# One TensorE piece, on alternating row halves, for the score products of both head groups of a chunk

## The chip, the cores and the metric

The kernel runs on one core of one Trainium2 chip. The metric is device time in microseconds (us) of one execution. The engines of the core work side by side and meet at semaphores: TensorE multiplies matrices (PE; its weight loads are shown apart as PEld), VectorE (DVE), ScalarE (ACT) and GpSimd (POOL) do element-wise work, and SyncE (SP) issues the transfers, which the DMA engines carry out.

## What is computed

Three layers follow one another. The first is a recurrent attention layer over 4 batches, 8 heads, 768 steps and head dimension 40. For each batch and head:

```
for t in range(S):
    m_new = maximum(f[t] + m, i[t]);  fs = exp(f[t] + m - m_new);  is_ = exp(i[t] - m_new)
    C = fs * C + is_ * outer(v[t], k[t]);   n = fs * n + is_ * k[t]
    y[t] = sigmoid(o[t]) * (C @ q[t]) / maximum(abs(n . q[t]), 1)
```

Its output, 3072 tokens by 320, goes through `((x @ w1) * (x @ w2) @ w3) @ w_out` (inner width 1024) and then through `max(x @ w1, x @ w2, x @ w3) @ w_out` (inner width 768). All is float32; the weights of the last two layers arrive as 64-bit floats and are converted on the chip.

## The kernel before

**Tiling of the first layer.** The 768 steps of a batch are cut into 9 chunks of 88 (the last has 64), and the 8 heads into 2 groups of 4. A unit `u` is one batch, one chunk and one head group: `u = 18 * b + 2 * c + g`, 72 units in all. Inside a unit the recurrence is computed in its parallel form: `s = k^T q` for every pair of steps of the chunk (`s`, 88 x 88 for each of 4 heads, in PSUM), times the decay factors `dd` (L610 writes the product into `pk`), and then `o = pk @ [v, 1, state]` (L625, in `outs`). `rest` takes the new state from `o` into `kv` of the unit two further on (L630), divides by the denominator (L643 to L646, into `y`) and multiplies by the gate (L651). When both groups of a chunk have their `y`, `x_cols` transposes it on TensorE (L666) and splits it into the high and low parts `xh` and `xl` that the second layer reads.

**Two ways of the product s.** Units below `NP = 28` use the direct way, on which the change bears: q and k of the unit arrive by one transfer as `raw`, 40 rows of data padded to 48 (L530), and four float32 matmuls with 40 rows each, one for each head, give `s` (L569); each shows as two weight loads and two matmuls in the trace. Later units split q and k into parts of lower precision and use L594; the change does not touch them.

**Buffers.** `s`, `o` (from unit 10 on) and the transposed `y` share two PSUM banks under the tag `aq`, in turn, by the order in which they are written down. `raw` has three buffers for units 0 to 9 (`raw0`) and two for the rest; those lie in a shared tile that the trace calls `misc`. A new tile waits until the old user of its buffer is done.

**The order of the work.** The program writes operations down with `P.op(engine, cost in ns, function, reads, writes)`; `Plan.run` then simulates all engines with these costs and with biases by kind of operation, and issues each engine's instructions in the order in which they start in that simulation. On the chip an engine's order is fixed: an instruction that waits holds up all behind it on its engine. That goes for SP too, which issues all transfers. The units are written down by `more()`: ten before the second layer begins (with three `fold` steps, L926, that combine two weight matrices on TensorE), then one at each of certain steps of the second and third layers (`a_step`, `b_step`, `c_step`, `d_step`, which make the long rows of L698 to L702, L765 to L769 and L784). So the units from 10 on are mixed into the matmuls of the second and third layers.

Of the kernel before, what the change touches and what calls it, by code (L numbers as in the profile page):

```python
# [8 lines left out]
F32 = mybir.dt.float32  # L9
# [7 lines left out]
B, H, S, D = 4, 8, 768, 40  # L17
L = 88
LP = 96
NCH = 9  # L20
# [8 lines left out]
NP = 28  # L29
NQ = 10  # L30
# [44 lines left out]
def act(n, psum=False):  # L75
    return (51 if psum else 93) + 0.8333 * n


def dve(n):
    return 69 + 1.0417 * n  # L80
# [200 lines left out]
def mlstm_moe_kernel(  # L281
# [21 lines left out]
    V, A, G, PE, SP = nc.vector, nc.scalar, nc.gpsimd, nc.tensor, nc.sync  # L303
    PS = bass.MemoryType.PSUM
    P = Plan()
# [41 lines left out]
    def view(t, shape, dt):  # L347
        n = 1
        for d in shape[1:]:
            n *= d  # L350
        v = t[0:shape[0], 0:n]
        if dt != F32:
            v = v.bitcast(dt)
        if len(shape) == 3:
            v = v.rearrange("p (a b) -> p a b", b=shape[2])
        elif len(shape) == 4:
            v = v.rearrange("p (a b c) -> p a b c", b=shape[2], c=shape[3])
        return v

    def new(key, shape, dt, tag):  # L360
        P.tile(key, tag, len(slots[tag]))
        made[key] = view(slots[tag][turn[tag] % len(slots[tag])], shape, dt)
        turn[tag] += 1
        if gates_done.get(tag):
            P.state[key][0][None] = gates_done[tag]
        return key

    def T(*key):
        return made[key]

    def dma(ns, fn, r=(), w=()):
        return P.op("D", ns, fn, r, w)
# [12 lines left out]
    def c3(t):  # L385
        return t.rearrange("p (c t) -> p c t", t=L)
# [21 lines left out]
    def f():  # L408
# [5 lines left out]
         r=[("g", "ff")], w=[("g", "git")])  # L414

    def f():
# [6 lines left out]
         r=[("g", "git")], w=[("g", "aug", 1)])  # L423

    def f():
# [7 lines left out]
        out=c3(T("g", "gft")), in0=c3(T("g", "gft")), in1=mp[:, 0:NCH].unsqueeze(2).to_broadcast([32, NCH, L]),  # L433
# [5 lines left out]
    for b in range(B):  # L439
        dma(141, lambda b=b: SP.dma_start(  # L440
            out=d_na[b].rearrange("c h t -> h c t"), in_=c3(T("g", "gft"))[b * 8:b * 8 + 8]
# [20 lines left out]
    for c in range(SIGN):  # L462
        dma(318, lambda c=c: SP.dma_start(out=sg0[0:LP, c], in_=og[0, c]), w=[("sg", (0, c))])
        sig.append(P.op("A", 360 + (1283 if c == 0 else 0), lambda c=c: A.activation(
            out=sg0[0:LP, c], in_=sg0[0:LP, c], func=AF.Sigmoid
# [13 lines left out]
    def ub(u):  # L479
        b, r = divmod(u, 18)  # L480
        return b, r // 2, r % 2, GL[r // 2], 128 if r > 1 else L
# [41 lines left out]
    def unit(u):  # L523
        if u < DUO:
            load(u + 2)
        b, c, g, n, r = ub(u)
        h0 = b * 8 + g * 4
        if u < NP:
            new(("raw", u), [48, 4, 2 * L], F32, "raw0" if u < NQ else "raw")
            dma(333, lambda: SP.dma_start(out=T("raw", u), in_=qk0[b, g, c]), w=[("raw", u)])  # L530
        else:
            new(("raw", u), [120, 2, 4, L], F32, "raw")
            dma(888, lambda: SP.dma_start(out=T("raw", u), in_=qk[b, g, c]), w=[("raw", u)])
        if L < r:
            new(("qq", u), [128, 4, L], F32, "qq")
            dma(174, lambda: SP.dma_start(out=T("qq", u)[80:128], in_=qk[b, g, c, 56:104, 0]),
                r=[("qqb", turn["qq"] % len(slots["qq"]))], w=[("qq", u)])
        new(("dd", u), [128, 4, n], F32, "dd")
        dma(464, lambda: SP.dma_start(
            out=T("dd", u)[:r], in_=d_na[b, c:c + 1, g * 4:g * 4 + 4, 0:n].to_broadcast([r, 4, n])  # L540
        ), r=[("dna", b)], w=[("dd", u)])
        if g == 0 and (b, c) >= (0, SIGN):
            gates(b, c)

        P.op("G", 735, lambda: G.tensor_tensor(  # L545
            out=T("dd", u)[:r], in0=am[:r, c, h0:h0 + 4].unsqueeze(2).to_broadcast([r, 4, n]), in1=T("dd", u)[:r],
            op=ALU.subtract,
        ), r=[("am", 0)], w=[("dd", u)])
        P.op("G", 460, lambda: G.affine_select(  # L549
            out=T("dd", u)[0:L], in_=T("dd", u)[0:L], pattern=[[0, 4], [1, n]], compare_op=ALU.is_ge, fill=-1e30,  # L550
            base=0, channel_multiplier=-1,
        ), w=[("dd", u)])
        P.op("A", act(4 * n) + (1283 if u == 0 else 0), lambda: A.activation(  # L553
            out=T("dd", u)[:r], in_=T("dd", u)[:r], func=AF.Exp
        ), w=[("dd", u)], after=sig)
        new(("pk", u), [128, 4, 128], F32, "pk")
        m = 128 if c < NCH - 1 else n
        if m > n:
            P.op("G", 415, lambda: G.tensor_tensor(  # L559
                out=T("pk", u)[:r, :, L:128], in0=T("kv", u)[:r, :, 0:40],  # L560
                in1=T("dd", u)[:r, :, n - 1:n].to_broadcast([r, 4, 40]), op=ALU.mult,
            ), r=[("kv", u, "k"), ("kvb", u % BUF["kv"]), ("dd", u)], w=[("pk", u, 0)])
        new(("s", u), [128, 4, n], F32, "aq")
        if u < NP:

            def f():
                raw = T("raw", u)
                for h in range(4):
                    PE.matmul(T("s", u)[:L, h], lhsT=raw[0:40, h, L:2 * L], rhs=raw[0:40, h, 0:n], start=True, stop=True)  # L569

            P.op("P", 720, f, r=[("raw", u)], w=[("s", u)])
        else:
            ks = kst[u % 2]
            new(("qs", u), [120, 4, n], F32R, "qs")
            P.op("A", act(4 * n), lambda: A.copy(out=T("qs", u), in_=T("raw", u)[:, 0, :, 0:n]),
                 r=[("raw", u)], w=[("qs", u)])
            P.op("A", act(4 * n), lambda: A.copy(out=ks, in_=T("raw", u)[:, 1]),
                 r=[("raw", u)], w=[("kst", u % 2, 1)])
            P.op("G", 889, lambda: G.tensor_tensor(
                out=T("qs", u)[0:40], in0=T("raw", u)[0:40, 0, :, 0:n], in1=T("qs", u)[0:40].bitcast(F32),  # L580
                op=ALU.subtract,
            ), r=[("raw", u)], w=[("qs", u)])
            P.op("V", dve(4 * n), lambda: V.tensor_tensor(
                out=ks[64:104], in0=T("raw", u)[64:104, 1], in1=ks[64:104].bitcast(F32),
                op=ALU.subtract,
            ), r=[("raw", u)], w=[("kst", u % 2, 1)], port=1)

            duo = u >= DUO
            if duo:
                new(("o", u - 1), [128, 4, 41], F32, "aq")  # L590

            def f():
                for h in range(4):
                    PE.matmul(T("s", u)[0:L, h], lhsT=ks[:, h], rhs=T("qs", u)[:, h], start=True, stop=True)  # L594
                if duo:
                    outs(u - 1)

            if duo:
                P.op("P", 1210, f, cols=300, r=[("qs", u), ("kst", u % 2), ("pk", u - 1), ("kv", u - 1)],
                     w=[("s", u), ("o", u - 1)])  # L600
            else:
                P.op("P", 390, f, cols=90, r=[("qs", u), ("kst", u % 2)], w=[("s", u)])
        if L < r:

            def scaled(e):
                e.tensor_tensor(out=T("pk", u)[64:128, :, 0:n], in0=T("qq", u)[64:128, :, 0:n],
                                in1=T("dd", u)[64:128], op=ALU.mult)

            P.op(("G", "V"), (889, dve(4 * n)), (lambda: scaled(G), lambda: scaled(V)), r=[("qq", u), ("dd", u)], w=[("pk", u, 1)], port=1)
        P.op("V", dve(4 * n), lambda: V.tensor_tensor(  # L610
            out=T("pk", u)[:L, :, 0:n], in0=T("s", u)[:L], in1=T("dd", u)[:L], op=ALU.mult
        ), r=[("s", u), ("dd", u)], w=[("pk", u, 1)])
        if u >= DUO:
            rest(u - 1)
            load(u + 2)
        if u + 1 < DUO or u == NU - 1:
            new(("o", u), [128, 4, 41], F32, f"ac{u % 3}" if u < 10 else "aq")
            P.op("P", 910 if m > n else 500, lambda: outs(u), cols=210, r=[("pk", u), ("kv", u)], w=[("o", u)])
            rest(u)
# [363 lines left out]
    def more():  # L983
        u = cur[0]
        if u < NU:
            unit(u)
            cur[0] = u + 1

    folds = [0]
# [75 lines left out]
def _lay(i):  # L1065
    import numpy as np

    f = np.float32
    q, k, v = i["q"], i["k"], i["v"]
    pad = lambda a: np.concatenate([a, np.zeros(a.shape[:-1] + (NCH * L - S,), f)], -1)  # L1070
    qk = np.stack([q, k], 2).reshape(B, 2, 4, 2, S, D).transpose(0, 1, 5, 3, 2, 4)
    qk = pad(qk).reshape(B, 2, D, 2, 4, NCH, L).transpose(0, 1, 5, 2, 3, 4, 6)
    eye = np.eye(D, dtype=f)
    qk0 = qk.transpose(0, 1, 2, 3, 5, 4, 6)
    qk0 = qk0.reshape(B, 2, NCH, D, 4, 2 * L)
    qk0 = np.concatenate([qk0, np.zeros((B, 2, NCH, 48 - D, 4, 2 * L), f)], 3)
    qk = np.concatenate([qk, qk[:, :, :, 0:24], qk, qk[:, :, :, 24:40]], 3)
    kvt = np.zeros((B, 2, NCH, LP, 4, 81), f)
    kvt[:, :, :, L:LP, :, 0:40] = eye[0:LP - L, None]
# [3 lines left out]
    for c in range(NCH):  # L1083
        n = GL[c]
# [58 lines left out]
```

## Time and profile before

| | |
|---|---|
| median of 3 runs | 730.17 us (728.78 to 731.63) |
| profiled execution | span 729.3 us from its first to its last instruction; its time outside the span is not in the rows |
| busy share | PE 96%, PEld 92%, DVE 60%, ACT 51%, POOL 42% |
| instructions | 12666, of them 4341 matmuls and as many weight loads |
| data moved | 78.84 MB, mean 108 GB/s |

PE busy is the time from a matmul's start to its modelled end; as they are pipelined, the pace is read from starts. Matmuls of line 569, which the change touches, start between 12.8 and 213.6 us.

### The profile page before, as it was taken

To read this page: it belongs to the slowest core of one execution; us is meant where nothing else is said; L and a number is where in the kernel's file an instruction comes from. 1 tells how busy PE (TensorE), PEld (TensorE's weight loads), DVE (VectorE), ACT (ScalarE), POOL (GpSimd) and SP (SyncE) were. 2 spreads that over 40 slices of the span, in tenths; PEclk is the share of its full clock that TensorE was granted. 3 is DMA by queue.
4 is the path that set the end of the run, shared out by engine and by line. 5 is a ranking of instruction groups with operands and counts; after the bars stand their busy time and mean duration, and the time that the engine had idled before them with its cause. 6 is when DMAs were issued, how large, how long until landed. Compare 5 with 4: busy or idle time off the path is not lost.

```text
span 729.3 us, 12666 instructions
## 1 busy us (share of the span) xinstructions
PE 699.4 (96%) x4341; PEld 674.3 (92%) x4341; DVE 437.0 (60%) x998; ACT 373.8 (51%) x697; POOL 308.3 (42%) x438
## 2 busy tenths in 40 slices
PE   1699999999999999999999999999999999999998
PEld 1677897889999999999999999999999999999998
DVE  4688876667766865866466676754747632233333
ACT  5968998689854355555343446545333222231311
POOL 1786755556646536664044456543406200000000
PEclk9978999999999999999999999999999999999999
DMA  7987887464433445543023445432305100000000
GB/s 207 251 247 226 233 230 219 146 185 157 148 88 102 117 111 148 139 124 87 12 76 85 109 121 153 113 83 69 88 1 112 49 1 27 1 1 1 1 27 28
DMA packets 50954, 78.84 MB, mean 108 GB/s; under 512 B 11882, under 2 KB 37930, under 8 KB 50890
## 3 DMA queue, kind: packets, MB, share of 16 engines
q1 hardware_dynamic: 50890, 78.04, 38.4%
q8 instruction: 34, 0.56, 0.3%
q14 instruction: 30, 0.25, 0.1%
HBM read 73.98 MB, written 4.03 MB: 107 GB/s over the span
## 4 chain that ended last, share of the span: by engine, by line
PE 84%; DMA 7%; DVE 3%; POOL 2%; issue 2%; SPq 1%; ACT 0%; POOLq 0%; DVEq 0%
PE wk L698 13%; PE wk L699 12%; PE wk L700 12%; PE ac L784 9%; PE aq L625 6%; PE wk L702 6%; PE wk L701 6%; PE ac L765 4%; PE ac L769 4%; PE wk L926 4%; PE ac L767 3%; DMA stg<-in_w3t 2%; PE aq L569 2%; PE aq L594 1%; DMA dd<-d_na 1%
## 5 line engine op out<-in xcount | busy, mean ns | idle before, releaser
L718 DVE TENSOR_TENSOR pl<-pr,ph 128x384 fp32r<-128x384 f32 (+1 forms) x91 | 60.8, 669 | 75.8 <-ACT ph L714 73.1
L714 ACT CAST ph<-pr 128x384 fp32r<-128x384 f32 (+1 forms) x114 | 57.8, 510 | 90.5 <-PE ac L784 43.9
L698 PE MATMUL wk<-xh,wch 128*128 128x384 f32 x288 | 99.5, 345 | 0.0
L700 PE MATMUL wk<-xl,wch 128*128 128x384 f32 x288 | 97.1, 337 | 0.0
L699 PE MATMUL wk<-xh,wcl 128*128 128x384 f32 x288 | 97.1, 337 | 0.0
L749 DVE TENSOR_TENSOR pr<-pr,wk 128x384 f32<-128x384 f32 (+1 forms) x98 | 52.8, 541 | 64.4 <-PE wk L702 57.8
L698 PE MATMUL wk<-xh,wah 128*128 128x384 f32 x256 | 90.9, 355 | 0.0
L718 POOL TENSOR_TENSOR pl<-pr,ph 128x384 fp32r<-128x384 f32 (+1 forms) x23 | 24.2, 1052 | 153.7 <-ACT ph L714 138.9
L699 PE MATMUL wk<-xh,wal 128*128 128x384 f32 x256 | 86.6, 338 | 0.0
L700 PE MATMUL wk<-xl,wah 128*128 128x384 f32 x256 | 86.5, 338 | 0.0
L545 POOL TENSOR_TENSOR dd<-am,dd 128x352 f32<-128x352 f32 (+2 forms) x72 | 57.5, 799 | 49.6 <-DMA dd<-d_na 48.8
L559 POOL TENSOR_TENSOR pk<-kv,dd 128x160 f32<-128x160 f32 (+1 forms) x64 | 38.7, 606 | 72.1 <-PE aq L625 64.9
L625 PE MATMUL aq<-kv,pk 128*128 128x41 f32 (+2 forms) x496 | 62.2, 275 | 2.1 <-POOL pk L559 1.4
L731 ACT COPY pr<-wk 128x384 f32<-128x384 f32 x64 | 30.5, 477 | 64.2 <-PE wk L702 64.1
L553 ACT ACTIVATE dd<-dd 128x352 f32<-128x352 f32 (+2 forms) x72 | 35.2, 492 | 52.3 <-POOL dd L549 51.7
L625 PEld LDWEIGHTS aq<-kv,pk 128*128 128x128 f32 (+2 forms) x496 | 57.4, 184 | 4.5 <-POOL pk L559 1.7
L651 POOL TENSOR_TENSOR misc<-misc 88x160 f32<-88x160 f32 (+1 forms) x62 | 41.5, 669 | 46.7 <-DVE misc L646 42.5
L746 ACT COPY pr<-wk 128x384 f32<-128x384 f32 x48 | 23.1, 482 | 70.5 <-PE wk L702 70.4
L733 DVE TENSOR_TENSOR pr<-pr,wk 128x384 f32<-128x384 f32 x64 | 35.2, 551 | 40.0 <-PE wk L702 35.7
L698 PEld LDWEIGHTS wk<-xh,wch 128*128 128x128 f32 x288 | 54.1, 188 | 0.1
L699 PEld LDWEIGHTS wk<-xh,wcl 128*128 128x128 f32 x288 | 54.2, 188 | 0.0
L700 PEld LDWEIGHTS wk<-xl,wch 128*128 128x128 f32 x288 | 54.0, 188 | 0.0
(133 smaller groups left out, 1729.5 us busy)
## 6 DMA issues: line engine op xcount, KB each, us to landing
misc<-in_qk SPq DMA_DIRECT2D x44, 330.0 KB
dd<-d_na SPq DMA_DIRECT2D x56, 176.0 KB
kv<-in_kv SPq DMA_DIRECT2D x72, 121.5 KB
stg<-in_w3t SPq DMA_DIRECT2D x13, 512.0 KB
stg<-in_wc SPq DMA_DIRECT2D x9, 512.0 KB
qq<-in_qk SPq DMA_DIRECT2D x64, 66.0 KB
misc<-in_og SPq DMA_DIRECT2D x31, 120.0 KB
out<-misc SPq DMA_DIRECT2D x23, 160.0 KB
```

The costliest lines, as they stand in the source:

```text
L545: P.op("G", 735, lambda: G.tensor_tensor(out=T("dd", u)[:r], in0=am[:r, c, h0:h0 + 4].unsqueeze(2).to_broadcast([r, 4, n]), in1=T("dd", u) ...
L625: PE.matmul(T("o", u)[:m, h], lhsT=T("pk", u)[:r, h, 0:m], rhs=T("kv", u)[:r, h, 40:81], start=True, stop=True)
L651: P.op("G", 485, lambda: G.tensor_tensor(out=yv(), in0=yv(), in1=sg(b, c).rearrange("p (h d) -> p h d", d=D)[:n, g * 4:g * 4 + 4], op=ALU.mult
L698: PE.matmul(p, lhsT=h_[:, kt], rhs=xh[:, kt], start=kt == 0, stop=False)
L699: PE.matmul(p, lhsT=l_[:, kt], rhs=xh[:, kt], start=False, stop=False)
L700: PE.matmul(p, lhsT=h_[:, kt], rhs=xl[:, kt], start=False, stop=False)
L701: PE.matmul(p, lhsT=r_, rhs=xh[:, 2], start=False, stop=False)
L702: PE.matmul(p, lhsT=r_, rhs=xl[:, 2], start=False, stop=True)
L714: P.op("A", act(n), lambda sl=sl: A.copy(out=T("ph", key)[:, sl], in_=T(*src)[:, sl]), r=[src + part], w=[("ph", key) + part])
L718: e.tensor_tensor(out=T("pl", key)[:, sl], in0=T(*src)[:, sl], in1=T("ph", key)[:, sl].bitcast(F32), op=ALU.subtract)
L749: P.op("V", dve(sl.stop - sl.start), lambda ps=ps, sl=sl: V.tensor_tensor(out=T(*sc)[:, sl], in0=T(*sc)[:, sl], in1=T(*ps)[:, sl], op=ALU. ...
L784: PE.matmul(T(f"ac{m}", (k, 1)), lhsT=src[:, m * 128:m * 128 + 128], rhs=w[:, o:o + DM], start=first_, stop=last_,)
```

## The change

One transfer now brings q and k of both head groups of a chunk: group 0 on rows 0 to 39 and group 1 on rows 64 to 103 of one tile of 104 rows, with zeros between. One TensorE piece then makes `s` of both units. It alternates between the groups: head 0 of group 0 from rows 0 to 39, head 0 of group 1 from rows 64 to 103, head 1 of group 0, and so on. Group 0 writes into one `aq` bank, group 1 into the other, and both are taken at once. The piece counts 800 in the plan, where each of the two counted 720; the transfer counts 720, where each counted 333. `more()` writes both units of a chunk down at the even call and nothing at the odd call. The number of matmuls is the same.

```diff
         if u < NP:
-            new(("raw", u), [48, 4, 2 * L], F32, "raw0" if u < NQ else "raw")
-            dma(333, lambda: SP.dma_start(out=T("raw", u), in_=qk0[b, g, c]), w=[("raw", u)])
+            if g == 0:
+                new(("raw", u), [104, 4, 2 * L], F32, "raw0" if u < NQ else "raw")
+                dma(720, lambda: SP.dma_start(out=T("raw", u), in_=qk0[b, c]), w=[("raw", u)])
...
-        new(("s", u), [128, 4, n], F32, "aq")
+        if u >= NP:
+            new(("s", u), [128, 4, n], F32, "aq")
         if u < NP:
-
-            def f():
-                raw = T("raw", u)
-                for h in range(4):
-                    PE.matmul(T("s", u)[:L, h], lhsT=raw[0:40, h, L:2 * L], rhs=raw[0:40, h, 0:n], start=True, stop=True)
-
-            P.op("P", 720, f, r=[("raw", u)], w=[("s", u)])
+            if g == 0:
+                for v in (u, u + 1):
+                    new(("s", v), [128, 4, n], F32, "aq")
+
+                def f():
+                    raw = T("raw", u)
+                    for h in range(4):
+                        for v, a in ((u, 0), (u + 1, 64)):
+                            PE.matmul(
+                                T("s", v)[:L, h], lhsT=raw[a:a + 40, h, L:2 * L], rhs=raw[a:a + 40, h, 0:n],
+                                start=True, stop=True,
+                            )
+
+                P.op("P", 800, f, r=[("raw", u)], w=[("s", u), ("s", u + 1)])
...
         if u < NU:
-            unit(u)
+            if u >= NP:
+                unit(u)
+            elif u % 2 == 0:
+                unit(u)
+                unit(u + 1)
             cur[0] = u + 1
```

The host lays q and k out to match, with 104 rows for each batch and chunk.

## Rows read from the trace of the kernel before

**Rows 1.** The page: span, and busy time by engine.

```profile
span 729.3 us, 12666 instructions
PE 699.4 (96%) x4341; PEld 674.3 (92%) x4341; DVE 437.0 (60%) x998; ACT 373.8 (51%) x697; POOL 308.3 (42%) x438
```

**Rows 2.** Windows: stretch, busy of PE, PEld, DVE, ACT, POOL, clock, DMA, GB/s.

```profile
0.00:24.00 24.00, 4.22 (x26) 3.66 (x26) 10.24 (x16) 13.50 (x19) 6.64 (x21) 1.00 0.82 221
24.00:60.00 36.00, 33.08 (x162) 28.05 (x162) 29.88 (x74) 29.15 (x43) 25.42 (x39) 0.81 0.87 246
60.00:112.00 52.00, 48.80 (x298) 43.37 (x298) 42.80 (x98) 47.44 (x76) 36.76 (x46) 0.97 0.80 227
112.00:216.00 104.00, 104.00 (x620) 93.49 (x620) 72.34 (x162) 85.68 (x145) 57.91 (x73) 1.00 0.53 158
216.00:730.00 514.00, 509.29 (x3242) 505.75 (x3241) 281.79 (x652) 198.03 (x418) 181.58 (x262) 1.00 0.26 71
```

**Rows 3.** Waits of TensorE, 60 to 112 us: us in total, times, longest.

```profile
PE aq L625 <- POOL pk L559: 1.4, 1, 1.4
PE aq L569 <- DVE kv L630: 0.8, 1, 0.8
PE aq L569 <- DMA misc<-in_qk: 0.7, 1, 0.7
PE aq L569 <- DVE pk L610: 0.3, 1, 0.3
```

**Rows 4.** Tile aq: duration ns min/median/max, first and last start.

```profile
L569 PEld LDWEIGHTS aq<-misc x144: 149/155/155, 71.0 to 213.5; 40*88 40x88 f32 x144
L569 PE MATMUL aq<-misc x144: 238/238/307, 71.0 to 213.6; 40*88 40x88 f32 x128, 40*88 40x64 f32 x16
L610 DVE TENSOR_TENSOR pk<-aq,dd x72: 412/520/524, 21.2 to 582.1; 88x352 f32<-88x352 f32 x64, 88x256 f32<-88x256 f32 x8
```

**Rows 5.** Timeline of TensorE around one unit: start, us, count at the end.

```profile
101.34 0.34 PE L702 MATMUL wk<-xl,war 128*128 128x384 f32 x1
101.61 0.85 PE L569 MATMUL aq<-misc 40*88 40x88 f32 x8
102.39 1.08 PE L625 MATMUL aq<-kv,pk 128*128 128x41 f32 x8
103.31 0.42 PE L698 MATMUL wk<-xh,wah 128*128 128x384 f32 x1
```

**Rows 6.** Timeline of the weight loads, same unit, without the first two.

```profile
101.76 0.55 PEld L569 LDWEIGHTS aq<-misc 40*88 40x88 f32 x6
```

**Rows 7.** Timeline of TensorE, an L625 piece with no L569 before it.

```profile
105.64 0.69 PE L769 MATMUL ac<-pl,wb 128*128 128x384 f32 x3
106.17 1.06 PE L625 MATMUL aq<-kv,pk 128*128 128x41 f32 x8
```

**Rows 8.** Windows of L569 alone: stretch, busy of PE and PEld, clock, DMA, GB/s.

```profile
60.00:112.00 52.00, 5.93 (x56) 4.88 (x56) 0.97 0.80 227
112.00:216.00 104.00, 9.38 (x88) 7.67 (x88) 1.00 0.53 158
```

**Rows 9.** Timeline of TensorE: units and folds between 27 and 116 us.

```profile
37.19 4.54 PE L926 MATMUL wk<-wof,w 128*128 128x320 f32 x8
...
41.66 1.49 PE L569 MATMUL aq<-raw 40*88 40x88 f32 x16
...
47.69 2.91 PE L569 MATMUL aq<-raw 40*88 40x88 f32 x16
...
111.91 2.35 PE L926 MATMUL wk<-wof,w 128*128 128x320 f32 x8
```

**Rows 10.** DMA issues of the whole run: count, KB each.

```profile
misc<-in_qk SPq DMA_DIRECT2D x18, 132.0 KB
...
raw<-in_qk SPq DMA_DIRECT2D x10, 132.0 KB
```

**Rows 11.** Waits of the transfer queue on SP, whole run.

```profile
SPq L530 <- PE aq L569: 9.1, 8, 2.1
```

More of the change, by code (lines that the diff above doesn't have):

```diff
@@ L1073, in _lay @@
     eye = np.eye(D, dtype=f)
-    qk0 = qk.transpose(0, 1, 2, 3, 5, 4, 6)
-    qk0 = qk0.reshape(B, 2, NCH, D, 4, 2 * L)
-    qk0 = np.concatenate([qk0, np.zeros((B, 2, NCH, 48 - D, 4, 2 * L), f)], 3)
+    pairs = qk.transpose(0, 2, 1, 3, 5, 4, 6).reshape(B, NCH, 2, D, 4, 2 * L)
+    qk0 = np.zeros((B, NCH, 104, 4, 2 * L), f)
+    qk0[:, :, 0:D] = pairs[:, :, 0]
+    qk0[:, :, 64:104] = pairs[:, :, 1]
     qk = np.concatenate([qk, qk[:, :, :, 0:24], qk, qk[:, :, :, 24:40]], 3)
```

## The prediction

> **What bounds the kernel now.** The page comes first: TensorE is busy for 96% of the span and nothing else for over 60%, apart from its own weight loads [rows 1]. The windows then show that this share is an average over stages with different limits. Up to 24 us TensorE mostly waits for the first transfers (4.22 of 24.00 us busy). From 24 to 60 it is busy for 33.08 of 36.00 us, but at a granted clock of 0.81, so part of that is spent at the lower of its two levels, while the DMA engines are at 0.87. From 60 to 112 it is busy for 48.80 of 52.00 us, with ScalarE close behind at 47.44. From 112 to 216 it has no idle time, and after that nearly none [rows 2]. The reader should see three cases: a us taken from TensorE's queue after 112 us should come off the end, between 60 and 112 only part of it, before 60 little.
>
> The waits of TensorE between 60 and 112 us are next: four, 3.2 us together, and three stand before the very instructions that change, for a transfer of q and k, for L610 and for L630, the last two because an `aq` bank was still in use [rows 3].
>
> Last the timeline, for what one unit's `s` costs TensorE at the full clock. Between the starts of L702 at 101.34 and of L625 at 102.39 lie 1.05 us [rows 5]. Where no `s` stands in between, three long matmuls and the step to L625 take 0.53 us, so a long one takes 0.18 [rows 7]. The unit therefore costs 1.05 - 0.18 = 0.87 us. Its pace within: six weight loads last 0.55 us in all, one lasts 0.155, so five steps take 0.395 and one 0.079 [rows 4, 6]. Eight at that pace are 0.63 us. The other 0.24 is entry and exit: 0.27 from L702 to the first L569, where 0.18 is usual, and the rest in a slow first step and a slow last one.
>
> What sets 0.079? L625 moves only 41 columns against loaded weights of 128, and its eight take 0.92 us, 0.115 each. L569 moves 88 against 88 [rows 5]. The pace follows the loaded columns (0.90 ns each in both), not the moved ones. So the loads set the pace, and overlapped matmuls alone would bring nothing: the loads of the two row halves must overlap too.
>
> **The change, part by part.**
>
> *Two pieces become one.* A pair costs 2 x 0.87 = 1.74 us before. One entry and exit always goes, 0.24 us. For the body, the trace of before has no two row halves at work at once, so it is bounded from both sides. If a load of one half waits for that of the other, 16 steps at 0.079 are 1.26, the pair 1.50, the saving 0.24. If the halves are independent, 8 double steps are 0.63, the pair 0.87, the saving 0.87. The nearest rows are the loads of L569 themselves, which share all their rows and so cannot settle it; but the pace by columns alone, 40 rows loaded as slowly per column as 128, says that the rows of the second half stand unused meanwhile. I take the independent case with a little lost at each change of half: 8 x 0.08 + 0.24 = 0.88, a saving of 0.86, and keep 0.24 as the other end.
>
> The Trainium skill, in TensorEngine Tiling (Array Packing), section Key Properties, says that different tiles of the array can load weights and multiply in parallel, and that a change of tiling mode drains the array. The entry of 0.27 where 0.18 is usual agrees with the second part; no run here shows the first. By the first alone the pair would cost what I take, and without it 1.50.
>
> *Where it counts.* At eight matmul records for a unit, units 10 to 16 lie before 112 us (56 records) and units 17 to 27 behind (88) [rows 8]. Five whole pairs come after 112: 5 x 0.86 = 4.3 us, in full, since TensorE has no idle time there. Units 10 to 17 are four pairs, 3.4 us. They lie in a stretch where ScalarE is at 91% and TensorE waits already; a shorter piece makes some of that wait longer. I take half, 1.7, between 0 and 3.4. Units 0 to 9 are five pairs. At the lower clock two units take 2.91 us, at the full clock 1.49 [rows 9]; half of that for each pair, 0.75 to 1.46, would be at most 7.3 in all. But the stretch hangs on transfers, on the conversion of weights by ScalarE and on the decay factors. I take 0.5. The other end is a loss: if less TensorE work there prolongs the lower clock over one more fold, that fold takes 4.54 in place of 2.35 us [rows 9], a loss of 2.2.
>
> *One transfer for two.* It brings 104 rows of 2816 bytes, 286 KB, for two of 132 KB [rows 10]: 22 KB more for each of 14 pairs. At 246 GB/s [rows 2] that is 0.09 us, below 0.5 for the five early pairs, hidden where the DMA engines have slack. If that cover is gone the 0.5 joins the early term, whose end of -2.2 is wide enough. SP issues 14 transfers fewer. It also waits for a free `raw` buffer (eight times, 9.1 us in all [rows 11]), and would now hold a buffer for two units, three or two buffers deep as before: the buffers reach further ahead in units, but the first `s` of a pair waits for data of both.
>
> The Trainium skill, in DMA: Bandwidth & Descriptors, section Why a DMA increments its semaphore by 16 and not by 1, speaks against this part: a transfer is spread over the largest number of engines up to 16 that divides its rows. By that rule 48 rows use 16 engines, three each, and 104 rows use 13, eight each, where two old transfers gave six. With that page's 27 GiB/s for an engine, two more rows are an estimated 0.2 us for a pair, 1 us over the five early ones. No row here shows an engine by itself.
>
> *Order and banks.* The joint piece takes both `aq` banks, so it waits for the older of their users in both: `o` of the last unit and, from the second bank, the transposed `y` of the last chunk. Before, the first of the two `s` needed one bank alone. Behind the waiting piece stands all of TensorE's queue. In return `o` of a pair waits only for its own L610 products, 0.52 us each [rows 4]. Writing two units down at one call also shifts the order that the plan makes, on all engines. No row prices that directly; the nearest are the four waits of 3.2 us [rows 3]. I take a third more of them, 1.0 us lost; the ends are a gain of 1 (the waits for the second piece of each pair fall away) and a loss of 4 (those waits come twice).
>
> *The sum.* -4.3 - 1.7 - 0.5 + 1.0 = -5.5 us. The profiled span of 729.3 becomes 723.8. The median of the runs is 0.9 above that span, so the forecast is 730.2 - 5.5 = 724.7 us. Its own range keeps the late term of 4.3: with 3.4 in the middle and 2 early and nothing lost it is 720.5, with 0.6 in the middle, none early and 2.7 lost it is 728.
>
> **The rivals.** *Loads take turns.* The halves do not overlap, the weight loads pass one after another, and the change does not do what it says. For it: loads set the pace already, and no row shows two in different rows at once. Against it: the unused rows. Only the entry and exit are saved: 5 x 0.24 + half of 4 x 0.24 = 1.7, less 1.0 for the order: 729.5 us.
>
> *The gain is given back.* The halves overlap, but between 60 and 112 us TensorE waits for what ScalarE, the transfers and the chain of units deliver. The term of 1.7 is gone, the early 0.5 too, and the waits come twice, 3.2 more: -4.3 + 3.2 = -1.1, 729.1 us. For it: 3.2 us of such waits today, ScalarE at 91%. Against it: other work is ready in the plan, and 93.8% busy says it mostly finds some.
>
> *Slower, by joint waits.* The piece stalls at TensorE's head for both banks and both groups' data. It decides from the point where the mean stall over the nine pairs after 60 us exceeds what is saved there, 6.0 us, or 0.67 a pair; today's waits are 0.3 to 1.4 [rows 3], so that is possible. At 1.2 a pair it costs 10.8 against 6.5 saved, +4.3: 734.5 us. Against it: five of the nine pairs lie where TensorE has not waited at all.
>
> **How the numbers follow.** A change of less than 0.5%, 3.65 us, cannot be told from none here. Chances: the forecast 0.52, loads in turn 0.26, given back 0.13, slower by stalls 0.09. The forecast case is under 726.5 us nine times in ten, which gives 0.47; the next two cases add 0.03 by their spread: faster 0.50. Slower is most of the last case and a trace of the others, 0.09. The rest, 0.41, is the same. The range of 720.5 to 732 holds the first three cases but for their tails, and leaves out the slower one and the best of the forecast case, some 0.15.
>
> **What the profile of the changed kernel would show.** If the forecast holds, 16 matmuls of the new `s` line lie within about 0.85 us from first start to the next operation's start at the full clock, and pairs of starts lie closer than 0.079 us. If that takes 1.4 us, the loads take turns. The waits of TensorE between 60 and 112 should stay near 3 us, those after 112 near none; each us more on the `s` line, waiting for L610, for L677 or L680 (which empty the bank of the transposed `y`) or for the transfer, is one given back. The granted clock of 24 to 60 us tells the early term. The prediction would be wrong through the body's pace above all, then through waits that the new order brings between 60 and 112.

## The result and the profile after

The changed kernel is slower: 736.85 us median (734.12 to 738.81), against 729.68 for the kernel before (728.78 to 731.63). The ratio is 1.0092, its 95% interval 1.0063 to 1.0121: a loss of 6.7 us by the ratio. The profiled execution is the shortest of the four, 734.12 us, with a span of 732.2, so its trace shows only a part of the loss. Two runs further down, one of 783.54 us of the kernel with 800 for 720 and one of 742.35 us of the refitted kernel before, were in a slower state and are left out of the ratios. Many lines have moved: the score matmuls stand on L575 now, L610 became L619, L625 L634, L630 L639, L666 L675, L698 to L702 became L707 to L711, and the bank of the transposed `y` is emptied by L686 on ScalarE and L689 on VectorE.

The page of the changed kernel answers to [rows 1]: span, then busy time by engine.

```profile
span 732.2 us, 12632 instructions
PE 690.8 (94%) x4341; PEld 664.1 (91%) x4341; DVE 447.2 (61%) x1005; ACT 370.9 (51%) x693; POOL 298.4 (41%) x433
```

TensorE is busy for 8.6 us less, with the same number of matmuls, and the span is 2.9 us longer. TensorE's work got shorter, and the end did not come sooner.

The timeline of TensorE around one joint piece of the changed kernel answers to [rows 5] (start, us, count at the end; the third line is the weight loads):

```profile
102.99 0.34 PE L711 MATMUL wk<-xl,war 128*128 128x384 f32 x1
103.25 0.86 PE L575 MATMUL aq<-misc 40*88 40x88 f32 x16
104.05 0.45 PE L707 MATMUL wk<-xh,wah 128*128 128x384 f32 x1
103.25 0.70 PEld L575 LDWEIGHTS aq<-misc 40*88 40x88 f32 x16 [0.25 <-DMA vs<-in_vs]
```

Sixteen matmul records last 0.86 us, where eight lasted 0.85 [rows 5], and sixteen weight loads of 0.149 to 0.155 each lie within 0.70, where six took 0.55 [rows 6]. Both units of a chunk cost what one cost, so the weight loads of the two row halves overlap as well as the matmuls. From L711's start to L707's start are 1.06 us, as 1.05 before for one unit: 0.87 us are saved for a pair.

The windows of the changed kernel answer to [rows 2] (stretch, busy of PE, PEld, DVE, ACT, POOL, clock, DMA, GB/s):

```profile
24.00:60.00 36.00, 30.91 (x159) 24.99 (x161) 29.46 (x71) 24.77 (x36) 24.58 (x39) 0.86 0.81 241
60.00:112.00 52.00, 45.19 (x292) 40.36 (x288) 44.68 (x99) 45.40 (x72) 36.16 (x48) 0.90 0.80 223
112.00:216.00 104.00, 100.89 (x625) 89.55 (x624) 78.84 (x165) 86.03 (x142) 53.49 (x70) 1.00 0.55 170
```

From 60 to 112 us TensorE has 6.8 idle us (52.00 - 45.19), before 3.2, and its granted clock is 0.90, before 0.97. From 112 to 216, where it had no idle time, it now has 3.1. In the early stretch the clock is a little higher, 0.86 for 0.81. The waits of TensorE between 60 and 216 us, which answer to [rows 3], name what it waits for (us in total, times, longest):

```profile
PE aq L675 <- POOL misc L660: 3.8, 5, 2.0
PE wk L707 <- ACT xh L686: 1.9, 1, 1.9
PE aq L575 <- DVE xl L689: 1.8, 2, 1.5
PE aq L634 <- DVE pk L619: 1.1, 3, 0.5
```

The largest is not the score piece. It is the transposes of L675, which stand in TensorE's order ahead of the gated `y` that they read. The score pieces' own wait is for L689. One is visible in the timeline of TensorE:

```profile
88.43 0.39 PE L575 MATMUL aq<-misc 40*88 40x88 f32 x2
90.30 1.16 PE L575 MATMUL aq<-misc 40*88 40x88 f32 x14 [1.49 <-DVE xl L689]
```

The piece begins, two matmul records (one head of group 0) run in the first bank, and then it waits for the second bank until VectorE has read the transposed `y`. VectorE's timeline shows why it is late:

```profile
86.84 1.73 DVE L885 SCALAR_TENSOR_TENSOR stg<-stg 128x512 int32<-128x512 int32 x1
88.49 0.85 DVE L727 TENSOR_TENSOR pl<-pr,ph 128x384 fp32r<-128x384 f32 x1
89.35 0.56 DVE L742 TENSOR_TENSOR pr<-pr,wk 128x384 f32<-128x384 f32 x1
89.82 0.43 DVE L689 TENSOR_TENSOR xl<-aq,xh 128x264 fp32r<-128x264 f32 x1
```

The split stands behind one weight conversion (L885) and two operations of the second layer (L727, L742) in VectorE's fixed order. So two theories offer themselves: the joint piece is to blame with its two banks, or the order that the plan made from the new input is.

### The profile page after: what moved, and what is told of

It is laid out like the page before. It is cut to its first block, busy times and chain, and to the rows that moved or that the text cites. A ratio compares the mean times of both kernels' runs of the same rounds, so it can differ in the third digit from the quotient of the medians.

```text
span 732.2 us, 12632 instructions
## 1 busy us (share of the span) xinstructions
PE 690.8 (94%) x4341; PEld 664.1 (91%) x4341; DVE 447.2 (61%) x1005; ACT 370.9 (51%) x693; POOL 298.4 (41%) x433
## 4 chain that ended last, share of the span: by engine, by line
PE 57%; DVE 0%; issue 0%; POOL 0%; ACT 0%; POOLq 0%
PE wk L707 9%; PE wk L708 9%; PE wk L709 9%; PE ac L793 7%; PE wk L711 5%; PE wk L710 4%; PE aq L634 4%; PE ac L774 3%; PE ac L778 3%; PE ac L776 2%; PE aq L603 1%; PE aq L675 1%; POOL dd L550 0%; DVE pl L727 0%; POOL misc L660 0%
## 5 line engine op out<-in xcount | busy, mean ns | idle before, releaser
L727 DVE TENSOR_TENSOR pl<-pr,ph 128x384 fp32r<-128x384 f32 (+1 forms) x94 | 62.0, 660 | 82.7 <-ACT ph L723 78.7
L707 PE MATMUL wk<-xh,wch 128*128 128x384 f32 x288 | 99.7, 346 | 0.0
L707 PE MATMUL wk<-xh,wah 128*128 128x384 f32 x256 | 90.7, 354 | 2.2 <-ACT xh L686 1.9
L727 POOL TENSOR_TENSOR pl<-pr,ph 128x384 fp32r<-128x384 f32 (+1 forms) x20 | 20.2, 1012 | 153.2 <-ACT ph L723 139.4
L560 POOL TENSOR_TENSOR pk<-kv,dd 128x160 f32<-128x160 f32 (+1 forms) x64 | 34.9, 546 | 78.7 <-PE aq L634 73.1
L634 PE MATMUL aq<-kv,pk 128*128 128x41 f32 (+2 forms) x496 | 61.0, 276 | 2.5 <-DVE xl L689 1.1
L634 PEld LDWEIGHTS aq<-kv,pk 128*128 128x128 f32 (+2 forms) x496 | 56.8, 185 | 4.7 <-DVE pk L619 2.2
L660 POOL TENSOR_TENSOR misc<-misc 88x160 f32<-88x160 f32 (+1 forms) x62 | 41.6, 671 | 47.4 <-DVE misc L655 36.7
L742 DVE TENSOR_TENSOR pr<-pr,wk 128x384 f32<-128x384 f32 x64 | 35.2, 551 | 38.7 <-PE wk L711 32.2
L879 ACT ACTIVATE stg<-stg 128x512 f16<-128x512 f32 (+2 forms) x41 | 52.5, 1279 | 3.7 <-DVE stg L871 2.6
L707 PEld LDWEIGHTS wk<-xh,wch 128*128 128x128 f32 x288 | 54.2, 188 | 0.1
```

The costliest lines, as they stand in the source:

```text
L634: PE.matmul(T("o", u)[:m, h], lhsT=T("pk", u)[:r, h, 0:m], rhs=T("kv", u)[:r, h, 40:81], start=True, stop=True)
L660: P.op("G", 485, lambda: G.tensor_tensor(out=yv(), in0=yv(), in1=sg(b, c).rearrange("p (h d) -> p h d", d=D)[:n, g * 4:g * 4 + 4], op=ALU.mult
L707: PE.matmul(p, lhsT=h_[:, kt], rhs=xh[:, kt], start=kt == 0, stop=False)
L727: e.tensor_tensor(out=T("pl", key)[:, sl], in0=T(*src)[:, sl], in1=T("ph", key)[:, sl].bitcast(F32), op=ALU.subtract)
L879: A.activation(out=sign, in_=tl()[:, :, 1].bitcast(F32), func=AF.Copy)
```

## The experiments

Differences are worked out from each ratio against the runs of the kernel before on the same chip, at about 730 us.

**The halves take turns.** The plan is that of the changed kernel; only the order inside the piece is another.

```diff
-                    for h in range(4):
-                        for v, a in ((u, 0), (u + 1, 64)):
+                    for v, a in ((u, 0), (u + 1, 64)):
+                        for h in range(4):
```

> The joint piece with the same plan, but first the four heads of group 0, then the four of group 1, so that the row halves take turns. The changed kernel shows 16 matmuls of a piece within 0.62 us where no stall cuts them. Theory 'the halves overlap only because they alternate': a whole piece takes 1.26 us at the full clock, and the time rises by up to 14 x 0.63 = 8.8 us where nothing hides it, at least by the 4 to 5 us of the pieces after 112 us: 741 to 745 us. Rival 'the halves overlap in any order': the piece stays near 0.7 us and the time at 735 to 738 us.

736.86 us, ratio 1.0087 (1.0060 to 1.0114), so no difference from the changed kernel. The piece did get longer, though not to 1.26 us, as the timeline of this kernel shows:

```profile
103.61 1.24 PE L575 MATMUL aq<-misc 40*88 40x88 f32 x16
```

One matmul lasts 0.24 us [rows 4], so the starts spread over 1.00 us, in place of 0.62. The time is the rival's and the piece is neither theory's: part of the overlap survives without alternation, and 0.38 us a pair, 3.4 us over the nine pairs from unit 10 on, made no difference beyond the noise of 2 to 3 us. In its windows TensorE is idle for 7.9 us between 60 and 216 us, in the changed kernel for 9.9, so the longer pieces took the place of waits in part.

**The two units written down together, without the joint piece.** The kernel before, with the changed `more()`:

```diff
-            unit(u)
+            if u >= NP:
+                unit(u)
+            elif u % 2 == 0:
+                unit(u)
+                unit(u + 1)
```

> The kernel before, with the two units of a chunk written down at one call; pieces and transfers stay apart. Theory 'the loss comes from the new order of the plan': most of the loss is there without the joint piece, 733 us or more, with waits of the transposes for GpSimd. Rival 'the loss comes from the two banks that one piece takes': 728 to 731 us, and no stall inside a score piece.

742.89 us, ratio 1.0168 (1.0145 to 1.0191): 12 us lost with no joint piece and no joint transfer. The waits of TensorE in this kernel between 60 and 216 us:

```profile
PE aq L569 <- DVE pk L610: 2.9, 2, 2.4
PE aq L625 <- DVE misc L646: 2.7, 1, 2.7
```

They stand at other places than in the changed kernel (the expected waits of the transposes are 0.5 us in all), but are of the same kind: an instruction at the head of TensorE's queue ahead of its data.

**Two transfers in place of one.**

```diff
-                dma(720, lambda: SP.dma_start(out=T("raw", u), in_=qk0[b, c]), w=[("raw", u)])
+                dma(333, lambda: SP.dma_start(out=T("raw", u)[0:48], in_=qk0[b, c, 0:48]), w=[("raw", u, 0)])
+                dma(333, lambda: SP.dma_start(out=T("raw", u)[56:104], in_=qk0[b, c, 56:104]), w=[("raw", u, 1)])
```

> The changed kernel, but each row half comes by its own transfer of 48 rows as before. Theory 'the larger transfer costs': the first o piece, which starts at 27.4 us instead of 23.9, starts 2 to 3 us sooner, and the time falls to 732 to 734 us. Rivals (order, banks): no change beyond noise, 735 to 738 us.

736.06 us, ratio 1.0086 (1.0057 to 1.0116). The first `o` piece does start sooner, at 25.89 us against 27.38, and the loss stays: it does not need the larger transfer. What the transfer costs by itself is not shown, since two counts of 333 in place of one of 720 are another input of the plan as well, and the next runs show what such an edit alone can do.

**One number of the plan.** Three kernels of before and two of the changed one with a cost in the plan that is a little different; every operation is the same, only the plan's result is not. That is more than the order: some operations may run on either of two engines, and the simulation picks the one. With the score cost changed, for example, VectorE makes 43 of the products of L606 in place of 39, and GpSimd 21 in place of 25. Below, "order" means both. First the score piece of before, 800 in place of 720:

```diff
-            P.op("P", 720, f, r=[("raw", u)], w=[("s", u)])
+            P.op("P", 800, f, r=[("raw", u)], w=[("s", u)])
```

> The kernel before, with one number changed: the plan counts 800 in place of 720 for a score piece of one unit. No instruction changes, only the order that the plan makes. Theory 'any change of the plan's input costs, since the biases were fitted to the old one': 733 us or more. Rival 'the loss belongs to this change': 729 to 731 us.

Ratio 1.0182 (1.0141 to 1.0222), a loss of 13 us. In the late window of this kernel (columns as above):

```profile
112.00:216.00 104.00, 98.34 (x547) 86.83 (x546) 66.50 (x147) 78.21 (x131) 51.10 (x65) 0.93 0.50 146
```

After 112 us TensorE is idle for 5.7 us and its clock falls to a mean of 0.93, where it was 1.00 [rows 2]. Then two numbers that have nothing to do with the score pieces, in both kernels: the gate multiply on GpSimd counts 500 in place of 485, and a group of eight long matmuls 1395 in place of 1387.

```diff
-        P.op("G", 485, lambda: G.tensor_tensor(
+        P.op("G", 500, lambda: G.tensor_tensor(
```

> The kernel before, with one number of the plan changed that has nothing to do with the score pieces: the gate multiply on GpSimd counts 500 in place of 485. Theory 'the order of before is a fitted one, and any shift of the plan's costs loses it': 735 to 745 us, as with the score cost (745.1). Rival 'only the cost of the score pieces is delicate': 729 to 731 us.

> The changed kernel with the same number changed, 500 for 485. Theory 'the order is arbitrary here too, and the joint piece itself gains': 735 to 741 us, and 3 to 7 us below the kernel before with the same number. Rival 'the joint piece itself loses (both banks at once)': level with or above it.

```diff
-        P.op("P", 1387, f, cols=3072, r=[("xh", key), ("xl", key), *r], w=[ps])
+        P.op("P", 1395, f, cols=3072, r=[("xh", key), ("xl", key), *r], w=[ps])
```

> The kernel before, the plan counts 1395 in place of 1387 for a group of eight long matmuls. Theory 'fitted order': 735 to 750 us. Rival: 729 to 731 us.

> The changed kernel with 1395 for 1387. Theory 'arbitrary order, and the joint piece gains': 3 to 7 us below the kernel before with the same number. Rival 'the joint piece loses by its banks': level with or above it.

| number changed | kernel before: us, ratio (interval) | changed kernel: us, ratio (interval) |
|---|---|---|
| none | 729.68, 1 | 736.85, 1.0092 (1.0063 to 1.0121) |
| gate 485 to 500 | 742.88, 1.0156 (1.0122 to 1.0189) | 742.47, 1.0169 (1.0137 to 1.0201) |
| group 1387 to 1395 | 736.48, 1.0084 (1.0064 to 1.0104) | 737.62, 1.0099 (1.0069 to 1.0130) |

A shift of 15 ns or 8 ns in one planned cost takes 11 or 6 us from the kernel before. Its 730 us depend on one order, and the loss from the change, 6.7 us, lies within what a change of the plan's input costs without it, 6 to 13 us. With the same number in both, the two kernels are level within about 3 us: the gain of 3 to 7 us that was expected of the joint piece does not show there, nor does a loss. As each of the four is one order out of many, two such pairs cannot settle a gain of a few us.

**New biases.** The plan has 69 biases, one for each kind of operation (the table BIAS). They were searched for anew, for both kernels; nothing else differs.

> The changed kernel with new values of the plan's 69 biases and nothing else: fitted to the new work by some 30,000 trials with the plan's own simulation, in which the order found was played again with every operation longer by about a tenth, so that it also has to stand delays. Theory 'the piece saves TensorE time, and the loss is the lost fit of the order': below the kernel before by 3 to 7 us, 723 to 727 us, with TensorE without waits again after 112 us. Rival 'the joint piece itself stalls (both banks, both groups)': still above 730 us, with stalls inside the score pieces.

> The changed kernel with the biases of a second search from another seed, which ended a little less well. Theory 'lost fit': again below the kernel before, 725 to 730 us. Rival 'stalls of the joint piece': above 730 us.

> Control: the kernel before with its 69 biases searched on from their old values in the same way and with as many trials. Theory 'its order is already fitted': 727 to 731 us. Rival 'any such search gains, with or without the joint piece': as far below 730 as the changed kernel with new biases.

The changed kernel came to 730.24 us, ratio 1.0001 (0.9982 to 1.0020), and with the second set to 730.35, 1.0017 (0.9994 to 1.0041). The control went up, to 733.88, 1.0055 (1.0034 to 1.0075), which neither theory of its expectation held. The same operations in a better order are thus 6.6 us faster, and the loss of the change is gone. The gain of 3 to 7 us that was expected below the kernel before is not there. From the page of the first refitted kernel, whose span is 727.4 us:

```profile
PE 686.4 (94%) x4341; PEld 660.3 (91%) x4341; DVE 448.3 (62%) x999; ACT 373.8 (51%) x700; POOL 299.9 (41%) x434
```

TensorE is busy for 13.0 us less than in the kernel before [rows 1], and the median time is the same. The windows after 60 us say where it stands:

```profile
60.00:112.00 52.00, 45.37 (x283) 41.19 (x283) 46.24 (x95) 44.31 (x71) 33.99 (x46) 0.93 0.73 213
112.00:216.00 104.00, 100.90 (x629) 90.16 (x627) 82.37 (x169) 89.42 (x151) 58.12 (x74) 1.00 0.57 172
```

Still 6.6 and 3.1 us idle. The expected order without waits was not found. The turns were tried in this order too:

> The changed kernel with the new biases, and the four heads of group 0 before the four of group 1, which made the piece 1.00 us long in place of 0.62 without a change of the time in the old order. Theory 'in an order without waits TensorE's time counts': 2 to 4 us above the same kernel with alternating halves (nine pairs by 0.38 us, all or the five late ones). Rival 'TensorE's time in these pieces is hidden in any order': no difference.

732.22 us, ratio 1.0030 (1.0016 to 1.0044), against 1.0001 for alternating halves: 2.1 us, give or take 1.7, for the 3.4 us of longer pieces. Here alternation is worth something.

**Further fitting, and another bank.** The second kernel of this pair takes the wait for the second `aq` bank away, and has biases of its own:

```diff
-                    new(("s", v), [128, 4, n], F32, "aq")
+                    new(("s", v), [128, 4, n], F32, "aq" if v == u else "wk")
```

> The changed kernel, its new biases searched on from those of the first search against more draws of delays. Theory 'the lost fit is the whole loss and can be won back beyond': 724 to 728 us. Rival 'the joint piece itself holds it at the level of before': 729 to 731 us again.

> The changed kernel with one line more changed: group 1's product goes into a bank of the tag wk (three banks of the long matmuls) and not into the second aq bank, so that the joint piece no longer waits for the reader of the transposed y; biases searched for in the same way. Theory 'the two aq banks are a price of the joint piece itself': 2 us or more below the other refitted ones, 724 to 728 us, with no wait for the split of the transposed y in the middle of a score piece. Rival 'the banks cost only in an unfitted order': no difference, 729 to 732 us.

733.29 us, 1.0050 (1.0030 to 1.0070), and 735.58, 1.0085 (1.0057 to 1.0112). Both missed. The biases that were fitted further are 3.6 us slower on the chip than those they started from, so fits of one and the same kernel differ by that much. The other bank was not faster, which speaks against the banks as a price of their own. The wait for the split is gone from its score pieces, but the largest wait between 60 and 216 us, 2.6 us, is again at one of them, for L639. As its order is another too, it doesn't prove it.

**TensorE's time alone, in the old order.** To price a us of TensorE without a new order, the score pieces of the kernel before were shortened and lengthened with its plan untouched.

```diff
-                for h in range(4):
+                for h in range(2 if u >= NQ else 4):
...
+                for h in (0, 1, 2, 3, 2, 3) if u >= NQ else range(4):
```

> The kernel before, its order untouched, but the score pieces of units 10 to 27 compute two of their four heads; the products of the other two are left out, so the output is not the layer's. That takes 4 x 0.078 = 0.31 us of TensorE from each of 18 units, 5.6 us in all, 3.4 of it after 112 us. Theory 'in the old, fitted order TensorE's time counts in full after 112 us and in part before': 3.4 to 5.6 us less, 724.5 to 726.5 us. Rival 'other engines set the pace there too': less than 2 us gained, 728 to 730 us.

> The counterpart: the order of before, and two of the four heads are computed twice in units 10 to 27 (nothing is left out, two products are written again). That adds 0.31 us to each of 18 units. Theory 'TensorE's time counts': 3.4 to 5.6 us more, 733.5 to 735.5 us. Rival 'other engines set the pace': less than 2 us more.

With two heads fewer 728.39 us, ratio 0.9968 (0.9954 to 0.9983): 2.3 us for 5.6 removed. With two heads twice 734.78, 1.0046 (1.0030 to 1.0062): 3.4 us for 5.6 added. So a us on TensorE is worth 0.4 when saved (0.2 to 0.6) and 0.6 when added. The first gained a little more than its rival allowed and less than its theory asked; the second is as its theory had it.

As the two kernels share one order, the same operation can be followed in both. First their windows from 60 to 112 us, then the L610 products of units 10 to 16 and of units 16 to 36 (first and last start), each time heads left out above heads twice:

```profile
60.00:112.00 52.00, 46.55 (x264) 39.47 (x262) 42.59 (x99) 49.33 (x79) 37.98 (x49) 1.00 0.83 236
60.00:112.00 52.00, 50.40 (x332) 44.93 (x331) 42.02 (x98) 47.74 (x78) 38.29 (x48) 1.00 0.85 233
L610 DVE TENSOR_TENSOR pk<-aq,dd x7: 412/510/521, 74.3 to 110.2; 88x352 f32<-88x352 f32 x6, 88x256 f32<-88x256 f32 x1
L610 DVE TENSOR_TENSOR pk<-aq,dd x7: 421/510/520, 74.7 to 111.4; 88x352 f32<-88x352 f32 x6, 88x256 f32<-88x256 f32 x1
L610 DVE TENSOR_TENSOR pk<-aq,dd x21: 412/514/522, 110.2 to 279.5; 88x352 f32<-88x352 f32 x17, 88x256 f32<-88x256 f32 x4
L610 DVE TENSOR_TENSOR pk<-aq,dd x21: 420/520/521, 111.4 to 286.1; 88x352 f32<-88x352 f32 x17, 88x256 f32<-88x256 f32 x4
```

At 0.079 us a step, eight records or 0.62 us lie between the two kernels for each unit. From unit 10 to 16 that makes 3.7 us, of which 0.8 arrived (35.9 against 36.7 us); TensorE is idle in this stretch for 5.5 us in place of 1.6. For units 17 to 27, 6.8 us lie between them, and 5.4 arrived (169.3 against 174.7 us). So a us of TensorE was worth about 0.2 before 112 us and 0.8 after, in one execution of each. The trace of the kernel before cannot be set beside them as simply: its granted clock from 60 to 112 us was 0.97 [rows 2], theirs 1.00.

## Why the prediction was wrong

*Two pieces become one* was right, and almost to the digit: a saving of 0.86 us a pair was taken, 0.87 was measured. The loads overlap; the rival in which they take turns fell. The Trainium skill, in TensorEngine Tiling (Array Packing), section Key Properties, says that different tiles can load and multiply in parallel; the trace agrees, with sixteen loads in 0.70 us.

*Where it counts* failed in part. The nine pairs after unit 9 were to give 4.3 after 112 us and 1.7 before it, 6.0 in all. At the measured 0.4 for each us saved, their 9 x 0.87 = 7.8 us are worth 3.1. By the two L610 rows the terms shrink to an estimated 0.7 before 112 us and 3.5 after it, 4.2 together. Both mechanisms hold in kind: where TensorE waits already, most of a saving turns into more waiting, and where it has no idle time, most of it arrives. Both terms were too large. The five early pairs were to give 0.5; no run priced them apart.

*One transfer for two* was taken as hidden. With two transfers the loss was the same, which agrees; as the plan's input was another there, the price of the transfer stays unmeasured.

*Order and banks* is the step that failed. It was priced at 1.0 us, at most 4, from the 3.2 us of waits in the old trace. From the result it must be about 10, an estimate: 6.7 us lost in spite of a gain worth 3 to 4. The nearest rows were the wrong ones. Waits in a trace show what the order costs that was made, not what another order would. That the order can cost as much is shown: 6 to 13 us in four kernels of before whose only edit is in the plan's input (a cost three times, the place where units are written down once), and 6.6 us won back in the changed kernel by biases alone. What the runs do not show is one edit inside the change that makes the order bad. The rival of joint waits had the sign and, with 734.5 us, nearly the time, but not the place: of 9.7 us of waits between 60 and 216 us only 1.8 are charged to a score piece, and most of the rest to transposes, `o` pieces and long matmuls that came up ahead of their data. The clock adds to them. At the lower level two units take 2.91 us, at the full one 1.49 [rows 9], so a mean of 0.90 in place of 0.97 over 52 us costs an estimated 3.6 us of TensorE's time, and 0.86 in place of 0.81 over the 36 us before gives 1.8 back. The clock stood at the lower level from 90.7 to 94.1 us, for one, right after the wait of 1.49 us shown above. The four runs of the changed kernel had mean granted clocks of 0.986, 0.984, 0.981 and 0.981, in the order of their times, 734.12 to 738.81 us. How much of the 6.7 us is the clock and how much is waiting alone was not separated. An order can cost without the clock: with the group at 1395 the kernel before lost 6 us at 0.986 to 0.993, where its control had 0.988 to 0.991.

What stays open is whether the joint piece is worth anything in an order fitted to it as well as the old one was to the old work. Two fits of the changed kernel ended 4 and 3 us below the one fit of the kernel before (ratios 1.0001 and 1.0017 against 1.0055), and the third, 1.0050, is level with it; with two shifted numbers the kernels were level too. A gain of 3 to 4 us fits the better two, but one fit of the kernel before and a spread of 3.6 us among the others do not show it. No order was found in which the changed kernel is clearly below 730 us.

## What to carry to other kernels

Where an order is made once by a plan and then fixed on every engine, price an edit of the plan's input by its order first: run the old instructions with one planned cost shifted by a per cent. If that alone moves the time by more than the edit can save, compare the edit only with the plan fitted again, and give the old kernel the same fit. And before a saving on the busiest engine is counted in full, shorten that engine's work in the old order by a known amount and see what of it arrives.

## What the runs showed of the hardware

Two row halves of TensorE's array loaded and multiplied side by side at no loss: 16 float32 matmul records of 40 rows took 0.86 us, and 8 of one half 0.85 [rows 5]. It happens in part even without alternation: with all of one half queued before the other, the starts spread over 1.00 us. One half after the other would need 15 steps of 0.079, 1.19 us, so matmuls of the second half began before those of the first had all begun. The Trainium skill, in TensorE: Matmul & The Clock Gate, Part 3 (The mechanism), says that matmuls start in the order of the program; for matmuls of different row halves, this measurement differs.
